# A new order for all 1302 steps of a fused delta-rule attention and bilinear FFN on one core

## The chip, the cores and the metric

One core of a Trainium2 chip runs the whole program. The metric is the device time of one execution in microseconds (us), as the median of several runs. Engines: TensorE (PE; its weight loads are listed as PEld), VectorE (DVE), ScalarE (ACT), GpSimd (POOL) and SyncE (SP), which issues nearly all DMAs.

## The reference: what is computed

Four batches of eight heads, 768 tokens, head size 48, all float32. The first half is a delta rule, token by token; the second half is an FFN whose hidden layer is a product of two projections, without an activation:

```python
for t in range(S):
    kt, vt, bt = (k_n[:, :, t], v[:, :, t], beta[:, :, t, None])
    y[:, :, t] = np.einsum('bhd,bhde->bhe', q[:, :, t], state)
    v_old = np.einsum('bhde,bhd->bhe', state, kt)
    state = state + bt[:, :, :, None] * np.einsum('bhd,bhe->bhde', kt, vt - v_old)
...
a = x @ w1
b = x @ w2
h = a * b @ w3
return (h @ w_out).astype(np.float32)
```

k_n is k divided by its norm. x is y with the heads side by side: 3072 tokens of 384 features; the hidden layer has 1024, and the weights come as 64-bit floats.

## The kernel before, in words

**Tiling.** The tokens of every head are cut into 12 chunks of 64. Within a chunk the recurrence becomes triangular: scores K Kt and K Qt, an inverse of a unit triangular matrix, and products with the state, which is handed from chunk to chunk. Two chunks make a pair j (or group u): their 128 blocks of 32 x 32 are inverted together, and their 512 tokens go through the FFN together. w3 and w_out are multiplied once into one matrix (w34), so the FFN is three products. The second product of the groups and the first two of the last group use a scheme with seven products of half size in place of eight, for which GpSimd forms sums of slabs and of weights.

**Steps.** Each piece of work is a Python generator, and each `yield` ends one step. The text `ORDER` (L39) names generators; a name that stands there for the n-th time runs that generator's n-th step. In this document V0.4 is step 4, counted from 0, of the generator V0. The names:

| name | line | what its steps do |
|---|---|---|
| P0-7, P8-23, P24-35 | L694 | one piece of w_out, of w3, of w1 and w2: .0 a DMA into one of five `raw` buffers (SP), .1 two passes on ACT, .2 two on DVE, .3 one on POOL, by which the 64-bit value becomes float32 |
| t, f | L745, L755 | transposes of w3 (TensorE, then a copy on ACT); products with w_out into w34 |
| k, q, v | L1088 | loads of a chunk; q0 and k0 are issued from ACT's queue, all others from SP's |
| K, Q (chunks 0, 1) | L329 | transposes of k and q on TensorE; copies on ACT and DVE |
| p, d (chunks 2-11) | L222, L318 | loads of k and q in 16 pieces, and their transposes on DVE |
| g, N | L263, L275 | squares of k on POOL and sums on DVE; norms on DVE, with a small product on TensorE |
| s | L356 | scores of a chunk: TensorE, then U and PT on DVE (for chunks 0 and 1 PT goes by ACT and POOL) |
| u | L407 | U to DRAM as blocks, four DMAs |
| V | L419 | a pair's inverse: .0 POOL, .1 load of the blocks (Ub), 31 steps of two DVE instructions each; for pairs 0 and 1 it works in PSUM, with two copies on ACT before (.2, .3; then .4 to .34 on DVE) and after (.35, .36), and .37 stores it |
| e | L475 | the corner blocks of a chunk: .0 loads, .1 DVE, .2 TensorE, .3 ACT, .4 TensorE, .5 ACT |
| n, c | L533, L542 | v times the norm on POOL; the chunk's chain with the state: TensorE and DVE by turns |
| y | L618 | .0 outputs of a chunk on TensorE, .1 copies into xT on ACT, .2 DMAs that fill the last rows of xT |
| b (first half of group 0), a0x to a4x | L771 | FFN, first products: .0 x w1 on TensorE, .1 copy on ACT, .2 x w2 on TensorE, .3 product on DVE |
| S, o, x | L993, L1009, L1059 | sums of slabs (POOL), second product (TensorE), result (ACT, DVE) and its stores (SP) |
| T, W, G5, E5 | L809, L836, L866, L887 | sums of weights (POOL) and of tokens (DVE), and the seven products of the last group |

**What sets the order.** `in_text_order` (L158) ties each engine's instructions to the order in which the list emits them; SP's DMAs too. An engine never overtakes: if the head of its queue waits, all behind it waits. Buffers go round in turn (`in_turn`, L137): five `raw`, four one-bank tiles `ps_f`, two two-bank tiles `ps_w`, three KQ, two xT, and so on; which buffer a step gets, and so whom it waits for, depends on how often the tag was asked for before it. DMAs take eight completion counters in turn, and a DMA waits until the one eight places before it in the list has landed.

Of the kernel before, what the change touches and what calls it, by code (L numbers as in the profile page):

```python
# [48 lines left out]
P30 t12 t14 t15 e0 t15 d3 f7 d3 f6 e0 P30 P21 e0 e0 P24 f7 s2 s2 e1 e0 s2 P24 e0 e1 V1 p4 s2 e1
P26 s2 e1 P25 d3 c0 P21 P30 u2 s3 c0 s3 P26 N1 P31 P24 y0 s3 s3 y0 c0 s3 s3 P25 t13 N1 e1 u3 P31  # L50
c0 P26 P31 P32 c1 V1 c1 e1 P25 V1 P27 c1 V1 c1 V1 V1 t13 V1 V1 V1 V1 V1 V1 y0 V1 P25 f7 f6 f6
P30 P32 P32 v2 V1 P27 s1 P31 V1 V1 y1 b3 b1 V1 b0 P32 P28 y1 b1 V1 b1 b3 P29 P27 b2 b3 y1 V1 P27
b1 b0 P29 P29 c1 a01 b2 a03 P28 V1 a01 a00 b3 P28 P29 a02 a02 a03 P35 P28 V1 a05 b7 a00 V1 V1 V1
V1 a06 P33 V1 b5 a05 b7 b0 V1 P34 V1 b5 V1 a06 V1 V1 V1 P34 k4 V1 P35 V1 g2 a00 V1 k5 a00 b0 V1
V1 g2 a04 P34 n2 p4 n2 a07 c1 a04 b2 b4 P33 b6 b2 P35 V1 g2 g2 P34 g2 e2 a07 g2 P33 e2 P35 c2 c2
e3 d4 a03 d4 a03 a01 P33 g2 b4 d4 g2 e2 b6 e2 a07 e2 b4 d4 T a01 T b4 e2 a07 c2 s4 p5 g2 c2 T g2
N2 V2 b6 p5 b6 s4 b5 s4 c2 a06 c2 a06 a04 v3 y2 d5 b5 d5 k6 s4 e3 d5 s4 y2 a02 a05 d5 s4 b7 a04
n3 S0 a02 a05 S0 s5 S0 u4 e3 s5 n3 s5 e3 b7 T o0 c3 c3 s5 g3 s5 S0 N2 N2 x0 e3 g3 e3 o0 s5 c3 c3
u5 o0 x0 V2 S0 x0 y3 V2 y3 S0 V2 S0 V2 S0 S0 V2 V2 V2 S0 g3 o0 S0 o0 S0 x0 V2 c3 o0 v4 y3 V2 V2
V2 x0 p6 V2 x0 V2 S0 a10 a10 S0 g3 S0 x0 V2 x0 S0 o0 x0 x0 p6 a14 V2 k7 a17 a17 a14 V2 V2 V2 a15  # L60
a16 V2 a16 a15 V2 g3 V2 V2 V2 V2 V2 v5 V2 x0 a13 V2 V2 V2 a17 a12 V2 a13 g3 V2 V2 g3 a17 c3 a14
a13 d6 d6 a11 V2 e4 n4 a12 e4 e4 c4 d6 V3 e4 a14 a10 n4 g3 d6 c4 e5 a11 e4 s6 g3 a13 e4 a12 p7
a10 c4 g3 N3 s6 c4 s6 a11 y4 n5 y4 c4 e5 a12 c4 a11 a15 c5 n5 e5 p7 a16 d7 d7 d7 d7 o1 c5 v6 a16
k8 g4 g4 e5 g4 p8 a15 g4 s7 s7 S1 e5 s7 S1 e5 x1 s7 s7 S1 s7 c5 o1 s6 S1 u7 c5 o1 s6 s6 u6 S1 S1
V3 S1 y5 c5 c5 V3 V3 V3 V3 V3 o1 S1 x1 k9 S1 y5 S1 y5 o1 S1 S1 x1 x1 V3 S1 S1 V3 c6 V3 S1 S1 V3
d8 o1 x1 x1 v7 a20 n6 x1 V3 a20 o1 x1 a23 V3 V3 x1 V3 x1 n7 a27 a24 d8 a26 V3 V3 V3 V3 x1 g4 V3
a23 V3 a25 V3 a27 a27 V3 a24 V3 V3 a26 a20 V3 g4 V3 p8 V3 V3 V3 V3 p9 V3 V3 a25 d8 n6 d8 g4 a20
a22 a22 a24 V3 c6 a27 a25 a24 a21 a21 e6 e6 e6 g4 e7 N3 e6 a25 N3 g4 s8 g4 N4 s8 e6 a22 s8 a26
e6 c6 c6 N4 s8 a26 s8 y6 a22 V4 p9 N4 S2 d9 e7 s8 a21 e7 y6 u8 d9 a21 e7 c6 a23 d9 p10 e7 d9 S2
c6 S2 s9 n7 a23 s9 e7 o2 s9 c7 s9 S2 s9 k10 S2 c7 x2 o2 c7 S2 S2 o2 u9 s9 V4 c7 V4 S2 y7 V4 V4  # L70
x2 V4 g5 g5 V4 p10 d10 y7 S2 x2 S2 o2 y7 V4 o2 x2 c7 V4 V4 S2 S2 V4 o2 a35 x2 x2 k11 x2 S2 V4 x2
S2 a35 v8 V4 S2 V4 V4 S2 V4 x2 n8 o2 a37 x2 V4 v9 V4 V4 V4 x2 a34 n8 V4 V4 a36 a30 V4 V4 V4 V4
V4 a37 V4 a34 a33 V4 g5 a33 a30 a32 a36 V4 V4 V4 V4 a34 a33 V4 V5 a32 e8 n9 c7 e8 a30 c8 a33 e8
e9 e8 g5 a35 a34 c8 a30 e8 g5 d10 a32 e9 g5 a32 g5 a36 e8 e9 S3 c8 a36 a35 a31 d10 d10 e9 a31 n9
c8 g5 c8 c8 g5 g5 e9 a31 s10 N5 e9 p11 s10 s10 a31 c9 a37 a37 p11 c9 y8 N5 v11 d11 S3 d11 d11 o3
v10 d11 s10 y8 s10 S3 u10 S3 s11 N5 s11 o3 s10 c9 s11 c9 s11 S3 x3 S3 s11 o3 S3 S3 y9 o3 s11 x3
S3 o3 u11 V5 S3 S3 V5 y9 V5 x3 n11 S3 x3 V5 V5 V5 S3 y9 S3 S3 V5 c9 V5 o3 x3 V5 x3 x3 V5 V5 x3
S3 a47 o3 x3 V5 V5 a47 x3 V5 V5 a47 n10 V5 a46 a40 a40 V5 a47 V5 a43 V5 a46 x3 a42 a45 V5 a42 V5
a41 a45 a43 V5 V5 V5 V5 V5 V5 a44 V5 a44 V5 a45 a41 V5 V5 V5 V5 c9 W W W W W W W W a42 e10 a40
e10 n11 a42 e10 a44 e10 c10 a45 n10 e11 e10 e11 c10 a43 e10 c10 c10 a40 e11 a41 a46 e11 c10 a44  # L80
S4 a43 e11 a41 S4 c10 o4 e11 a46 c11 x4 S4 S4 y10 o4 c11 c11 S4 y10 S4 S4 S4 S4 S4 c11 o4 y11 o4
x4 S4 S4 S4 o4 y11 x4 x4 o4 S4 x4 x4 S4 y11 S4 x4 G5 x4 E5 x4 o4 x4 E5 x4 E5 E5 S5 E5 E5 S5 E5
E5 S5 o5 S5 S5 S5 o5 S5 S5 S5 x5 S5 S5 S5 o5 o5 x5 S5 S5 S5 o5 S5 o5 x5 x5 o5 x5 x5 x5 x5 x5 x5
x5 x5 x5 x5
"""


# [1117 lines left out]
```

## Time and profile before

| | us |
|---|---|
| median of 3 runs | 587.72 |
| lowest, highest | 586.81, 589.62 |
| the profiled execution's span, first to last instruction | 592.1 |
| TensorE busy in it | 540.8 |
| VectorE, ScalarE, GpSimd busy in it | 378.9, 159.2, 192.8 |

The profiled execution gives no time besides its span, which is 4.4 us above the median of the runs. Its mean granted TensorE clock is 0.971.

When some steps started in it, by matching the trace's instructions with the list:

| step | engine | start, us |
|---|---|---|
| K0.0, first transposes | TensorE | 7.5 (ends 10.9) |
| N0.0, first norms | DVE | 26.3 |
| s1.5, last write of U for pair 0 | DVE | 39.4 |
| V0.4, first step of the first inverse | DVE | 52.2 |
| V0.34, its last; V0.37, its store | DVE; SP | 84.2; 88.4 |
| e0.2, first corner product | TensorE | 97.2 |
| c0.0, first product of the chain | TensorE | 103.8 |
| V1.4, V1.34 | DVE | 125.1, 153.7 |
| e2.2 | TensorE | 165.7 |
| a10.0 | TensorE | 212.4 |
| a23.2 | TensorE | 345.6 |
| W.0, first of the weight sums for the last group | POOL | 476.1 |

How to read a page: busy shares by engine come first, then the span in 40 slices, where a digit is tenths of busy time (PEclk: tenths of the granted clock), then DMA queues, then groups of instructions. A line number is one of the kernel printed above. The waits are given as who waited for whom: total us, how often, and the longest.

### The profile page before, as it was taken

The page shows a single profiled execution, that of the slowest core. Times are in us where ns is not written, and L with a number is a line of the kernel's source. Part 1 is how long each engine was busy: PE and PEld are TensorE (multiplying, and loading weights), DVE is VectorE, ACT ScalarE, POOL GpSimd, SP SyncE. Part 2 cuts the span into 40 slices and gives each one's busy share as a digit, 9 for nine tenths or more (in the row PEclk, how much of TensorE's full clock was granted, in tenths as well). Part 3 has the DMA queues.
Part 4 walks back from the last instruction along what each step waited for, and adds up shares of the span by engine and source line. Part 5 has one row for each costly group of instructions (what it writes and reads, how often), then busy time and mean ns, then how long its engine had stood idle before and what let it go on. Part 6 is the DMA issues. An engine that isn't in the chain of part 4 may idle for free.

```text
span 592.1 us, 19305 instructions
## 1 busy us (share of the span) xinstructions
PE 540.8 (91%) x8268; PEld 393.3 (66%) x8268; DVE 378.9 (64%) x872; ACT 159.2 (27%) x337; POOL 192.8 (33%) x240
## 2 busy tenths in 40 slices
PE   2469889788989999999999989999999999999997
PEld 2456455667878874558854659644688445988897
DVE  3796897678986579674787544874855943325432
ACT  4666354453412202121210222011122112311100
POOL 7563543032453701207121025022051071501441
PEclk9879998779999999999999989999999999999999
DMA  9979997677857445563453344625332040010001
GB/s 245 198 163 268 196 182 140 127 162 154 133 78 101 99 83 107 83 98 56 113 99 75 56 64 86 125 60 78 58 64 79 27 89 4 3 41 27 1 1 53
DMA packets 219508, 57.32 MB, mean 97 GB/s; under 512 B 206656, under 2 KB 212800, under 8 KB 219424
## 3 DMA queue, kind: packets, MB, share of 16 engines
q1 hardware_dynamic: 215232, 55.31, 47.2%
q10 hardware_dynamic: 4192, 0.79, 1.0%
q8 instruction: 65, 1.06, 0.8%
q14 instruction: 19, 0.16, 0.1%
HBM read 43.88 MB, written 11.01 MB: 93 GB/s over the span
## 4 chain that ended last, share of the span: by engine, by line
PE 60%; SPq 15%; DMA 14%; DVE 6%; issue 3%; ACT 1%; POOL 0%; DVEq 0%; ACTq 0%
PE ps_f L778 29%; PE ps_f L1032 14%; SPq L229 6%; PE ps_w L550 4%; DMA raw<-in_moe_w_dram 4%; PE ps_f L897 3%; PE ps_w L651 3%; PE ps_w L897 3%; DMA Ub<-Ud 2%; DMA ktok<-in_k_dram 2%; PE ps_w L497 2%; SPq L201 2%; DMA Ud<-U 2%; DVE tb L439 1%; SPq L683 1%
## 5 line engine op out<-in xcount | busy, mean ns | idle before, releaser
L778 PE MATMUL ps_f<-xT,w2s 128*128 128x512 f32 (+1 forms) x288 | 112.2, 535 | 2.2 <-issue 2.2
L778 PE MATMUL ps_f<-xT,w1s 128*128 128x512 f32 (+1 forms) x288 | 107.0, 524 | 2.8 <-DMA xT<-xT 2.8
L1004 POOL TENSOR_TENSOR ab<-ab 128x256 f32<-128x256 f32 x96 | 67.0, 728 | 90.2 <-DVE ab L794 60.9
L778 PEld LDWEIGHTS ps_f<-xT,w1s 128*128 128x128 f32 x288 | 53.9, 190 | 48.7 <-issue 42.9
L778 PEld LDWEIGHTS ps_f<-xT,w2s 128*128 128x128 f32 x288 | 53.4, 191 | 44.6 <-issue 41.5
L1032 PE MATMUL ps_f<-w,ab 128*128 128x192 f32 x376 | 66.6, 330 | 0.2 <-issue 0.2
L1032 PEld LDWEIGHTS ps_f<-w,ab 128*128 128x128 f32 x376 | 61.1, 190 | 3.8 <-issue 2.9
L790 ACT COPY ab<-ps_f 128x512 f32<-128x512 f32 (+1 forms) x48 | 23.6, 517 | 130.9 <-PE ps_f L778 119.6
L439 DVE TENSOR_TENSOR tb<-Vb,Ub 128x31 f32<-128x31 f32 (+15 forms) x124 | 44.8, 361 | 19.6 <-DMA Ub<-Ud 16.3
L1032 PE MATMUL ps_f<-room,ab 128*128 128x192 f32 x272 | 48.0, 329 | 1.0 <-DVE room L1063 0.8
L444 DVE TENSOR_TENSOR Vb<-Vb,tb 128x31 f32<-128x31 f32 (+15 forms) x124 | 45.0, 363 | 4.3
L758 PE MATMUL ps_f<-w2s,w3T 128*128 128x384 f32 x128 | 45.8, 513 | 0.2 <-ACT w3T L752 0.2
L1032 PEld LDWEIGHTS ps_f<-room,ab 128*128 128x128 f32 x272 | 44.1, 190 | 1.8 <-issue 1.3
L672 ACT COPY xT<-ps_w 48x256 f32<-48x256 f32 x96 | 30.4, 365 | 55.0 <-PE ps_w L651 54.5
L269 POOL TENSOR_TENSOR sq<-ktok 128x384 f32<-128x384 f32 x24 | 20.7, 868 | 68.6 <-DMA ktok<-in_k_dram 62.3
L794 DVE TENSOR_TENSOR ab<-ab,ps_f 128x512 f32<-128x512 f32 (+1 forms) x48 | 27.7, 590 | 16.9 <-PE ps_f L778 16.7
L536 POOL TENSOR_TENSOR vtok<-vtok,n 128x384 f32<-128x384 f32 x24 | 20.3, 855 | 50.1 <-DMA vtok<-in_v_dram 50.1
L758 PEld LDWEIGHTS ps_f<-w2s,w3T 128*128 128x128 f32 x128 | 25.0, 201 | 16.9 <-issue 2.4
L366 PE MATMUL ps_w<-KQ 48*64 48x128 f32 x384 | 30.1, 293 | 1.7 <-DVE PT L396 1.7
L372 PE MATMUL ps_w<-KQ 48*64 48x64 f32 x768 | 30.5, 232 | 0.1
L714 POOL TENSOR_TENSOR w<-w,raw 128x512 uint32<-128x512 uint32 x16 | 20.8, 1305 | 27.7 <-ACT raw L707 9.0
L372 PEld LDWEIGHTS ps_w<-KQ 48*64 48x64 f32 x768 | 27.3, 145 | 0.3 <-ACT KQ L346 0.2
(155 smaller groups left out, 782.2 us busy)
## 6 DMA issues: line engine op xcount, KB each, us to landing
raw<-in_moe_w_dram SPq DMA_DIRECT2D x16, 512.0 KB, 6.5
vtok<-in_v_dram SPq DMA_DIRECT2D x24, 192.0 KB, 4.4
raw<-in_moe_w_dram SPq DMA_DIRECT2D x24, 192.0 KB, 4.6
out_dram<-osb SPq DMA_DIRECT2D x46, 96.0 KB, 2.3
ktok<-in_k_dram SPq DMA_DIRECT2D x44, 96.0 KB, 4.2
raw<-in_moe_w_out_dram SPq DMA_DIRECT2D x8, 384.0 KB, 4.4
Ud<-U SPq DMA_DIRECT2D x48, 64.0 KB, 3.2
Ub<-Ud SPq DMA_DIRECT2D x6, 512.0 KB, 3.9
```

The source lines that it names most:

```text
L229: sync.dma_start(out=dst[quarter(2 * e + j), :, :, tb, 0:nd].rearrange("t b a d -> t (b a) d"), in_=src.rearrange("b (a e) t d -> e (b a) ...
L366: pe.matmul(ps[half(z), 0, n : n + 128], lhsT=x[:, 0, :], rhs=x.rearrange("p j t -> p (j t)"), start=True, stop=True,)
L372: pe.matmul(ps[half(z ^ j), 1, n + C * j : n + C * j + C], lhsT=x[:, 0, :], rhs=x[:, j, :], start=True, stop=True,)
L439: dve.tensor_tensor(out=tv, in0=V[:, 0 : s + 1, s : s + 1].to_broadcast([P, s + 1, n]), in1=U[:, s, s + 1 : BS].unsqueeze(1).to_broadcast( ...
L444: dve.tensor_tensor(out=o, in0=o, in1=tv, op=ALU.subtract)
L672: act.copy(out=xT[f, p:NP:2, b : b + NR, cc, :].rearrange("p a r t -> p r a t"), in_=pyv[f, z, b : b + NR],)
L758: pe.matmul(ps[:, 0:DM], lhsT=w3Ts[jc, kc // 4][:, kc % 4 * P : kc % 4 * P + P], rhs=wo[:, kc], start=(kc == 0), stop=(kc == KF - 1),)
L778: pe.matmul(ps[:].rearrange("p b c t -> p b (c t)"), lhsT=w[:, m, js], rhs=x[:, m, :, c0:c1].rearrange("p b c t -> p b (c t)"), start=(m = ...
L794: dve.tensor_tensor(out=t, in0=t, in1=ps, op=ALU.mult)
L897: pe.matmul(acc[i, w, name], lhsT=w12_sums[w][b][:, P * i : P * i + P], rhs=x_sums[u][x], start=new, stop=True, skip_group_check=not new,)
L1004: pool.tensor_tensor(out=o_, in0=x_, in1=y_, op=op)
L1032: pe.matmul(ps[b][:, b, :], lhsT=abs_[u, HF * f + i][:, t0 : t0 + P], rhs=ws_[w][:, i], start=first and i == 0 and (b == 0 or n == "F"), s ...
```

## The change: the list

`ORDER` is replaced by another order of the same 1302 names, each as often as before. Every generator still runs its own steps in their order, so a step of one name never passes another of the same name; what changes is how the 271 generators are interleaved, and with it each engine's queue, the order on SP's and ACT's DMA queues, and which buffer and which counter a step gets. Nothing else in the file differs, except that the list is one line shorter, so that line numbers behind it fall by one.

The beginnings of the two lists, to the start of the first inverse:

```diff
 ORDER = """
-V0 P0 k0 beta P18 P13 P0 P18 P0 P0 P18 P18 g0 P11 beta P13 K0 K0 P11 P10 q0 P10 P3 k1 P11 P13 K0
-beta P12 g0 P3 K0 g0 K0 g0 P13 K1 g0 P8 P12 g0 K1 K1 P11 P9 Q0 Q0 g0 Q0 P10 P12 g0 Q0 Q0 g0 k2
-K1 s0 g0 P9 P10 P8 N0 K1 q1 P2 s0 N0 P3 Q1 s0 P12 p2 g1 Q1 P2 N0 s0 s0 Q1 P9 Q1 P8 Q1 g1 s0 P3
-s0 t2 t2 t3 s1 P5 P8 P2 g1 s1 P2 P1 s1 s1 t3 P9 P5 s1 P4 s1 P5 u0 P5 s1 d2 P1 P4 t1 u1 t0 P6 t4
-P7 t1 t10 P1 t0 t5 V0 t4 P14 g1 V0 P1 t10 P6 f1 t5 V0 d2 P4 P6 V0 V0 V0 P7 V0 P7 V0 P16 P14 V0
...
+P13 q0 k0 K0 P13 g0 Q0 g0 P11 P11 P12 P10 P11 P11 P13 P13 K0 k1 P3 g0 g0 K0 g0 P10 V0 P10 P0 g0
+P12 K0 K0 Q0 Q0 Q0 P12 K1 K1 P10 Q0 s0 P0 P18 P18 P3 P12 t4 P0 g0 g0 t4 P18 P3 P0 K1 beta q1 beta
+P3 g0 K1 g0 beta N0 s0 K1 Q1 Q1 P8 s0 p2 P18 P4 t5 Q1 Q1 P8 P8 P6 t5 k2 Q1 t2 t10 s0 s0 s0 P6 d2
+d2 s1 s0 s1 s1 s1 P6 s1 s1 P8 P1 P4 P1 u0 t3 P1 P1 P6 t2 P2 t3 P4 P4 t10 P9 P9 P9 u1 P7 P2 P2 P2
+P7 N0 P7 P5 P5 P5 V0 V0 V0 t0 V0 V0 V0 V0 N0 V0 V0 P19 P19 P19 P5 g1 V0 V0 f2 P7 f2 P16 p2 P9 V0
...
```

Other places that the prediction speaks of, each engine's steps alone, old list first:

```
SP, up to e0.0     P21.0 P24.0 p3.0 P26.0 p3.1 V0.37 P30.0 e0.0
                   P20.0 P26.0 P21.0 p3.1 V0.37 P30.0 P24.0 e0.0
TensorE, to c0.0   e0.2 f7.1 e0.4 s2.3 e1.2 c0.0
                   f7.1 e0.2 e0.4 s2.3 t13.0 c0.0
SP, up to V1.37    P33.0 P34.0 k4.0 k5.0 p4.1 V1.37
                   v2.0 k4.0 P34.0 P35.0 p4.1 V1.37 k5.0
SP, before y3.2    V2.1 x0.2 v4.0 y3.2 p6.0
                   V2.1 p6.0 y3.2
TensorE, to s7.3   a16.2 o1.0 s7.0 e5.4 s7.3
                   a15.2 e5.4 s7.0 a11.2 s7.3
TensorE, to a23.2  c6.2 N4.1 s8.3 y6.0 a21.2 e7.2 c6.4 a23.2
                   e7.2 N3.1 c6.2 a24.2 c6.4 y6.0 a23.2
SP, before y7.2    V4.1 p10.1 x2.2 y7.2
                   V4.1 v9.0 x2.2 y7.2
POOL, W            all eight before n11.1, n10.1 and S4.0
                   three behind S4.0, five between S4.14 and S4.15
```

## The prediction

> **What bounds the kernel now.** I read the page's busy shares first, then TensorE's own waits, then busy time in stretches, and last the rows around the longest wait of the second half.
>
> ```profile
> span 592.1 us, 19305 instructions
> PE 540.8 (91%) x8268; PEld 393.3 (66%) x8268; DVE 378.9 (64%) x872; ACT 159.2 (27%) x337; POOL 192.8 (33%) x240
> PEclk9879998779999999999999989999999999999999
> q8 instruction: 65, 1.06, 0.8%
> ```
>
> TensorE is busy for 540.8 of 592.1 us. The last row, of the DMA queues, has packets, MB and share. The list changes no instruction, so all that an order can win or lose is in the other 51.3 us and in the slices with a lower granted clock.
>
> ```profile
> 0.00:20.00 20.00, 6.47 (x138) 5.50 (x140) 8.34 (x14) 9.36 (x15) 13.91 (x28) 1.00 1.03 228
> 20.00:40.00 20.00, 12.77 (x350) 11.34 (x342) 18.91 (x40) 12.39 (x22) 11.04 (x10) 0.74 0.87 187
> 160.00:180.00 20.00, 17.85 (x505) 14.95 (x496) 16.85 (x41) 2.41 (x5) 10.15 (x11) 1.00 0.51 78
> 220.00:240.00 20.00, 20.00 (x48) 8.80 (x47) 17.55 (x40) 3.32 (x6) 4.75 (x7) 1.00 0.50 99
> 340.00:350.00 10.00, 7.75 (x139) 3.50 (x137) 5.37 (x8) 2.89 (x8) 2.20 (x3) 0.83 0.53 77
> ```
>
> Columns after the length: busy PE, PEld, DVE, ACT, POOL, clock, DMA share, GB/s. Adding 20 us less PE over the first ten stretches gives 40.8 us of idle before 200 us; 10.5 us are left after it, 4.0 of them the tail. Later stretches are full (20.00 of 20 at 220 to 240) but for single waits. Early, VectorE is as full as TensorE (18.9 of 20 at 20 to 40; 115.3 against 115.9 of the 140 us from 20 to 160), and what TensorE multiplies there comes from it. So two places are priced: the start, along VectorE's chain, and single waits later.
>
> ```profile
> PE ps_f L336 <- DMA ktok<-in_k_dram: 7.4, 4, 4.9
> PE ps_f L778 <- DMA xT<-xT: 2.8, 3, 1.5
> PE ps_f L778 <- issue: 2.2, 1, 2.2
> 342.80 0.58 PE L550 MATMUL ps_w<-X,ktok 64*48 64x48 f32 x35
> 345.62 0.70 PE L778 MATMUL ps_f<-xT,w2s 128*128 128x512 f32 x1 [2.25 <-issue]
> ```
>
> The first block of names is who TensorE waited for; "issue" means for nothing that the profile shows.
>
> **The start, to e2.2.** I write V0.4 for call 4 (from 0) of the step V0. I add the trace's durations step by step in each list's order and follow the queue that is late. First K0.0, which needs k0's four DMAs. DMAs take eight completion counters in turn, and each waits for the one eight places before: P13's, ninth in the old list, started at 4.93, when k0's first had landed at 4.91. In the new list q0 and P13 are ahead, so k0's third DMA waits for P13 and its fourth for q0's second. q0 has k0's bytes and its old place, and k0's last landed at 8.9; with 0.65 us to issue and 4.1 to 5.9 us to land (k0's first and last) k0 is complete at 13.7 to 15.5. If q0 landed in 4.1 us it would be 10.4. I take 14, since the loads now beside it are as many as then; it was 8.9.
>
> VectorE now has g0.1, which needs k0, at its head (it had 3.0 us of weight pieces ahead of K0.1). From g0.0 on POOL (0.8) it starts at 14.9 with 15.9 us of work before N0.0: 30.8 against 26.3. Behind s0.1 stands P8.2, whose ACT half is queued behind s0.2 and two copies (0.6 each): 2.5 us of idling. But s1.5, the last write of U, ends after 25.7 us of VectorE work and not 28.8: 14.9 + 25.7 + 2.5 = 43.1 (40.1 before). On SP u1 stands behind P9.0, whose buffer is free after P8.3, and POOL does P8.3 after s1.3. From s1.1 (41.5) that is 0.6 of ACT, two times 1.3 of POOL and 0.3 of SP: 45.0. With u1's four issues (2.2 as u0's, 4.0 as its own), 1.7 to land and 5.8 from V0.1 to V0.4, V0.4 starts at 54.7 to 56.5, against 52.2; both rows are as near, so I take the middle, 55.6, +3.4.
>
> From there the new list makes it up, because SP is less in the way:
> - V0.4 to V0.34: 32.2 us of work against 30.8 (N0.2 is in it), and 1.6 of waiting as before: ends 89.4, +4.8.
> - V0.37, the store of the inverse, went out 3.8 us after V0.34 because SP was in p3.1 until 88.4. Now only two ACT copies (0.6 each) lie between: 90.8, +2.4.
> - e0.1 ends 12.1 us of VectorE work behind V0.34 (10.9 before), so e0.2 starts at 101.6, +4.4. From e0.2 to c0.0 took 6.6 with f7.1 (2.78) in the middle; without it two ACT pairs (1.2 each) and 0.7 of TensorE leave 5.0: c0.0 at 106.6, +2.8.
> - c0.0 to the end of s3.3 took 9.5, with 2.0 of "issue" before y0.0; 8.2 by the durations: +1.5. Through u3, P27 and V1.1, V1.4 comes at 125.7, +0.6.
> - V1.4 to V1.34 has 26.0 us of work against 27.0, and 2.0 of waiting as before: 153.7. V1.37 waited 3.9 us behind p4.1 with k5 ahead of it; k5 (2.7) is now behind it. But e2.1 ends 12.2 us of VectorE work behind V1.34 (10.3 before): 165.9, and e2.2 starts at 166.0, against 165.7.
>
> TensorE has 126.7 us of work before e2.2 in both lists. So this term is **+0.3 us**; with k0 at 10.4 every number of the chain is some 3 us earlier (-2.7), and if nothing is made up after V0.4 it is +3.4.
>
> **Instruction fetch.** 16,536 records of TensorE and 65 packets of q8 make 254 to a packet. Packets in dense stretches begin 4.3 to 4.6 us apart (98.4, 103.0, 107.3, 111.7, 116.3), some 58 a us. The old list holds 71 a us over 16.3 us of TensorE work from e6.2 to c6.4; behind it is the 2.25 us wait, and the six passes of a23.2 then took 4.54 us where others take 2.77 (clock 0.83 in 340 to 350). In the new list e6.2 to a23.2 has 60 a us. I take the whole, 2.25 + 1.77: **-4.0 us**. Bounds: -4.8 if e3.4's 0.8 goes too, and +4.0 for one new wait of that kind, since e7.2 to y6.0 is still 88 a us over 7.5 us.
>
> [...]
>
> **Single waits later.** y3.2, which makes the last rows of xT, has p6.0 (4.1 us on SP) ahead of it now, but SP waits for nothing there and is through by 203; what counts is that a10.0 now comes 6.3 us of TensorE work after y3.0, not 9.1. y3.2 started 2.0 after y3.0's end, took 3.7 and lands in 2.0: 7.7, so 1.5 us of waiting. For the third group the distance falls from 10.0 to 9.3: +0.3. Before a35 TensorE waited 0.5, with p10.1 ahead of y7.2 on SP; it is behind it now: -0.5. s7.3 waited 0.92 for VectorE with 0.57 us of TensorE work between; now a11.2 (2.77) covers it: -0.9. Together **+0.4**; bounds -1.4 (no xT wait) and +3. The later inverses have windows of TensorE work of 48.6, 53.5, 48.9 and 48.9 us from scores to corner (49.9, 48.6, 47.6, 47.6 before) and 1 to 3 us more VectorE work in them; spare time was 2 to 5 us, so I cost them at nothing, +2 if that cover is gone. W, moved from 476 to just before E5, puts 10.2 us on POOL where it was idle for 29.0 of the 40 us from 500 to 540: nothing.
>
> **Sum.** 0.3 - 4.0 + 0.4 = -3.3 us on 592.1. Unprofiled runs have a median of 587.7, 4.4 less; the change is carried over unscaled: 584.4.
>
> **Rivals.**
> 1. *The wait stays* (the change doesn't do what it says for fetches): "issue" falls elsewhere, or at y6.0 again. For: 88 a us there, and a stretch of 86 a us (c10.4 to y10.0) that passed without a wait, so density alone doesn't decide. Against: 60 instead of 71 over the longer stretch. 0.3 + 0.4: 588.4.
> 2. *Slower: the late first load is not made up.* VectorE's two inverses pass V0.4's +3.4 on to e2.2, and xT's 1.8 come on top, with no fetch gained: +5.2, 592.9. For: VectorE's 115.3 of 140 us. Against: SP's 3.8 and 3.9 us of delay, which are in the trace. It decides from about 90 on: if V0.34 ends later than that and V0.37 more than 3 us behind it.
> 3. *More*: k0 at 10.4 us: -2.7 instead of 0.3: 581.4.
>
> **How the numbers follow.** The forecast with rival 3: 0.46 (0.34 and 0.12). Rival 1: 0.26. Rival 2: 0.28. About 0.5%, 2.9 us, is what a measurement here can tell from no change. The likeliest is 584.4. The lower end adds up the good bounds (-2.7 - 4.8 - 1.4 = -8.9, 578.8) and some 4 us for the idle of the start that I priced by one chain only: 575. The upper end is rival 2 with one unhidden inverse (+2): 595.
>
> **What would show it.** Right: K0.0 ends at 14 to 16, V0.4 starts at 55 to 57, V0.37 goes out within 2 us of V0.34, e2.2 near 166, no "issue" wait near y6.0 and a23.2 at about 2.8 us, an xT wait of 1 to 2 us before a10.0. Wrong: TensorE's idle before 200 us outside 38 to 43 us, or idle after 200 us above 10.5.

## The result, and the profile after

The new list is slower: a median of 611.99 us (606.68 to 613.16, five runs) against 588.87 (586.81 to 589.62, five runs), a ratio of 1.037, 95% interval 1.033 to 1.042. The forecast was 584.4, and its range ended at 595. The profiled execution spans 605.0 us, and is the fastest of the five; the four others span 609.0 to 611.5. One execution in the experiments below, the profiled one of old_to_e2 (917 us at a clock of 0.57), was disturbed and is left out of every ratio.

The page of the new list, in the lines that answer to those shown of before (busy shares, granted clock in 40 slices, the queue of instruction fetches):

```profile
span 605.0 us, 19284 instructions
PE 545.6 (90%) x8268; PEld 393.8 (65%) x8268; DVE 387.6 (64%) x872; ACT 159.1 (26%) x337; POOL 193.2 (32%) x240
PEclk9766999789899999999999999999999999999999
q8 instruction: 65, 1.06, 0.7%
```

The same 8268 matmul records took 545.6 us instead of 540.8, and VectorE's 872 took 387.6 instead of 378.9. So the 12.9 us between the two profiles are 4.8 us of longer TensorE records and 8.1 us of more idling (49.6 us of idle before 200 us, 40.8 before; 9.7 behind it, 10.5 before). That is an account of TensorE's time and not yet of causes. The longer records go with the granted clock: it is 0.50 for 47.8 us in sum, 34.1 before (not counting the end), and its digits fall to 6 and 7 in the second to fourth slice, where before had 8 and 7 in the second and third. The stretches (columns as in the prediction):

```profile
0.00:20.00 20.00, 4.32 (x128) 3.77 (x128) 3.47 (x5) 3.59 (x5) 8.43 (x21) 1.00 0.79 184
20.00:40.00 20.00, 11.26 (x204) 9.77 (x204) 16.17 (x37) 11.18 (x20) 10.67 (x11) 0.57 0.77 164
140.00:160.00 20.00, 15.97 (x128) 12.68 (x127) 15.27 (x39) 9.20 (x22) 5.31 (x5) 0.91 0.72 133
340.00:350.00 10.00, 10.00 (x322) 6.41 (x322) 4.04 (x9) 4.06 (x7) 0.00 (x0) 1.00 0.30 49
```

In the first 20 us VectorE now works 3.47 us (8.34 before) and TensorE 4.32 (6.47). From 20 to 40 the clock is 0.57. 340 to 350, where before had its long wait, is full. TensorE's own waits:

```profile
PE ps_f L335 <- DMA ktok<-in_k_dram: 14.7, 3, 12.9
PE ps_f L335 <- ACT KQ L345: 8.5, 3, 5.0
PE ps_f L777 <- ACT ab L789: 3.4, 2, 2.8
PE ps_f L748 <- issue: 2.6, 1, 2.6
PE ps_w L549 <- issue: 2.3, 1, 2.3
```

The wait for k grew from 7.4 to 14.7 us; the second and third row had no counterpart; "issue" is there again, at other lines. The one at L748 is t10.0's, and it is no wait for nothing: in the list's order of the `ps_f` banks t10.0 gets one that Q1.0 had, and it starts 0.1 us after ACT's second copy of Q1 has ended (41.39 against 41.29). The wait for xT is gone.

Where the time was lost, by start of a step (us); the last column is a second profile of the same list (608.5 us, the run `new_again` below):

| | before | forecast | after | again |
|---|---|---|---|---|
| K0.0, end | 10.9 | 14 to 16 | 17.4 | 17.4 |
| N0.0 | 26.3 | 30.8 | 35.0 | 35.0 |
| s1.5, end | 40.1 | 43.1 | 48.6 | 48.6 |
| V0.4 | 52.2 | 55.6 | 61.4 | 61.1 |
| V0.34, end | 84.6 | 89.4 | 94.4 | 94.2 |
| V0.37 | 88.4 | 90.8 | 95.5 | 95.9 |
| e0.2 | 97.2 | 101.6 | 109.7 | 109.4 |
| c0.0 | 103.8 | 106.6 | 115.6 | 115.3 |
| V1.4 | 125.1 | 125.7 | 135.6 | 137.4 |
| V1.34, end | 154.1 | 153.7 | 166.6 | 168.5 |
| e2.2 | 165.7 | 166.0 | 178.0 | 180.1 |
| span | 592.1 | 588.8 | 605.0 | 608.5 |

9.2 us are lost at V0.4, 12.3 at e2.2, 12.9 at the end: the loss between these two profiles is the start's, and nothing behind it is won or lost on balance. The two profiles of the new list agree within 0.4 us up to c0.0. The old start has a spread of its own: in old_to_e2_b below, the same first 476 names reach V0.4 at 51.7 and e2.2 at 163.5, so that the loss up to e2.2 is 12 to 17 us by the pair of profiles one takes.

The medians differ by more than the two profiles, by 17 to 23 us. A run's time is 1.7 us above its span, so the old list's profile, 592.1, stands for some 593.8, above the five runs given here, and the new list's is the shortest of its five.

### The profile page after: what moved, and what is told of

It is laid out like the page before. It is cut to its first block, busy times and chain, and to the rows that moved or that the text cites. A ratio compares the mean times of both kernels' runs of the same rounds, so it can differ in the third digit from the quotient of the medians.

```text
span 605.0 us, 19284 instructions
## 1 busy us (share of the span) xinstructions
PE 545.6 (90%) x8268; PEld 393.8 (65%) x8268; DVE 387.6 (64%) x872; ACT 159.1 (26%) x337; POOL 193.2 (32%) x240
## 4 chain that ended last, share of the span: by engine, by line
PE 71%; DVE 9%; DMA 6%; SPq 4%; ACT 3%; issue 3%; POOL 1%; POOLq 0%; ACTq 0%; DVEq 0%
PE ps_f L777 29%; PE ps_f L1031 18%; PE ps_w L549 6%; DMA raw<-in_moe_w_dram 4%; PE ps_w L650 4%; PE ps_f L896 3%; PE ps_w L896 3%; PE ps_w L496 3%; PE ps_w L365 2%; DVE tb L438 2%; PE ps_w L371 2%; DVE Vb L443 2%; DMA qperm<-in_q_dram 1%; SPq L697 1%; SPq L228 1%
## 5 line engine op out<-in xcount | busy, mean ns | idle before, releaser
L777 PE MATMUL ps_f<-xT,w2s 128*128 128x512 f32 (+1 forms) x288 | 113.5, 536 | 2.8 <-ACT ab L789 2.8
L777 PE MATMUL ps_f<-xT,w1s 128*128 128x512 f32 (+1 forms) x288 | 108.9, 526 | 2.3 <-ACT w L764 0.7
L777 PEld LDWEIGHTS ps_f<-xT,w1s 128*128 128x128 f32 x288 | 53.8, 191 | 45.9 <-issue 39.5
L438 DVE TENSOR_TENSOR tb<-Vb,Ub 128x31 f32<-128x31 f32 (+15 forms) x124 | 46.2, 373 | 12.7 <-DMA Ub<-Ud 9.3
L757 PE MATMUL ps_f<-w2s,w3T 128*128 128x384 f32 x128 | 48.1, 528 | 6.2 <-POOL w2s L713 4.5
L443 DVE TENSOR_TENSOR Vb<-Vb,tb 128x31 f32<-128x31 f32 (+15 forms) x124 | 47.2, 381 | 4.3
L377 DVE TENSOR_TENSOR U<-ps_w,wt 128x512 f32<-128x512 f32 x24 | 16.6, 690 | 26.3 <-PE ps_w L371 22.0
```

The costliest lines, as they stand in the source:

```text
L438: dve.tensor_tensor(out=tv, in0=V[:, 0 : s + 1, s : s + 1].to_broadcast([P, s + 1, n]), in1=U[:, s, s + 1 : BS].unsqueeze(1).to_broadcast( ...
L443: dve.tensor_tensor(out=o, in0=o, in1=tv, op=ALU.subtract)
L757: pe.matmul(ps[:, 0:DM], lhsT=w3Ts[jc, kc // 4][:, kc % 4 * P : kc % 4 * P + P], rhs=wo[:, kc], start=(kc == 0), stop=(kc == KF - 1),)
L777: pe.matmul(ps[:].rearrange("p b c t -> p b (c t)"), lhsT=w[:, m, js], rhs=x[:, m, :, c0:c1].rearrange("p b c t -> p b (c t)"), start=(m = ...
```

## The experiments

The results are given as ratios to the kernel before, measured beside each, since its own median moved between 589.9 and 592.5.

| run | what | ratio, 95% interval |
|---|---|---|
| new_again | the new list | 1.031, 1.025 to 1.037 |
| old_first_30 | 30 old names first | 1.021, 1.014 to 1.028 |
| old_head_new_rest | 139 old names first (to V0.4) | 1.012, 1.006 to 1.018 |
| old_to_e2, old_to_e2_b | 476 old names first (to e2.2) | 1.0045, 1.001 to 1.008; 1.003, 1.000 to 1.007 |
| new_head_old_rest | 130 new names first (to V0.4) | 1.030, 1.023 to 1.038 |
| k0_first | k0 P13 q0 | 1.030, 1.023 to 1.036 |
| k0_q0_late | and q0 behind P13.1 | 1.028, 1.023 to 1.034 |
| k0_first_q0_sp | k0 first, q0 from SP | 1.026, 1.019 to 1.033 |
| head_pieces_first | and VectorE's pieces first | 1.025, 1.020 to 1.030 |
| loads_ahead | P29.0, P28.0 ahead of y1.2 | 1.029, 1.024 to 1.033 |
| head_and_loads | the last two in one | 1.015, 1.010 to 1.019 |
| new_w3_no_pool | eight GpSimd passes left out | 1.031, 1.028 to 1.035 |
| before_warm | old list, 86 products in idle time | 1.028, 1.023 to 1.033 |
| before_warm_128 | 128 products | 1.013, 1.005 to 1.020 |
| before_shift_88 | 22 small products | 1.023, 1.018 to 1.028 |
| before_warm_aligned | 86 and 42 small ones | 1.006, 1.003 to 1.008 |
| new_shift_88 | new list, 22 small products | 1.048, 1.042 to 1.054 |

### Which part of the list loses

```diff
-ORDER = the new list
+ORDER = the first n names of the old list, then the names left over, in the new list's order
```

(n = 30, 139, 476; new_head_old_rest is the same the other way round, with 130 new names; new_again has the new list.)

> The new list once more, unchanged, for its spread: its profiled execution took 605.0 us, its other four 609.0 to 611.5. If the start decides (the rounds of q0 and k0 on the DMA queues differ from run to run), a second profile differs from the first before V0.4 and is the same length behind it. If something later does, V0.4 starts at 61.4 within 1 us again and the difference lies behind it. Median 607 to 613.

> The first 139 names of the old list (to the start of the first inverse, V0.4), then the rest in the new list's order. Theory 'the start is carried': the late V0.4 (+9.2 us) goes straight through to the end, and what is left is what the new list lost behind it (+3.6 in the two profiles): V0.4 at 52 to 53, span about 596, median 590 to 595. Rival 'the rest loses': most is lost behind V0.4 whatever the start was: V0.4 at 52 to 53, but e2.2 at 172 or later and a median of 600 or more.

> The first 130 names of the new list (to V0.4), then the rest in the old list's order. Theory 'the start is carried': V0.4 at 60 to 62, span about 601, median 597 to 602. Rival 'the old rest makes it up' (what the prediction had assumed of the new one): e2.2 within 4 us of 165.7, median 588 to 592.

> The first 30 names of the old list (the loads of w_out's and w3's first pieces, k0, beta, q0 and k1, and the passes on P0, P18, P11 and P13 that stand ahead of the squares of k), then the rest in the new list's order. Theory 'who stands at VectorE's head': in the new list VectorE's first instruction needs k0 and stands idle for 16.5 us with weight pieces behind it; with the old first names it does 4 to 5 us of them before k0 is there, so V0.4 comes at 52 to 55, and the median at 596 to 601. Rival 'the rest of the head': the order from N0.0 on (P8.2, P1, P4, P9, P2, P7, P5 ahead of V0.4) is late by itself: V0.4 at 57 or later and a median of 603 or more.

> The first 476 names of the old list (to e2.2), then the rest in the new list's order: what the two later terms of the prediction are worth by themselves. Theory 'they hold': -4.0 for the fetch wait before a23.2 and +0.4 for single waits, so about 588 in the profile and a median 2 to 4 us below the kernel before. Rival 'the fetch wait moves': a new wait for nothing of 2.1 to 2.4 us at c10.4 (where the new list has it in three profiles of three) takes half of it back: median within 2 us of before. Rival 'the middle loses more': E5.0 later than 531 and a median above before.

> The same list as old_to_e2 (first 476 names old, then the new order), for its profile: the median there was 2.9 us above before (ratio 1.0045), where the prediction's two later terms gave -3.6. Theory 'the fetch wait moves': no wait before a23.2, a new one of about 2.3 at c10.4, E5.0 within 2 us of 528.5. Rival 'xT and inverses': a10.0, e4.2, e6.2, e8.2 or e10.2 fall behind old by 2 us or more at one place, by a wait for VectorE or a DMA.

Measured. new_again: the two profiles are the same up to V0.4 (61.1), have the same idle time of TensorE (55.3 and 55.4 us without the tail), and differ by 3.4 us of longer TensorE records: the clock was low for 58 us instead of 48, not counting the end (mean granted clocks of 0.952 and 0.961). So the difference lies behind V0.4, as the second expectation had it; that it goes with the clock, neither had.

With more of the old list in front, the loss shrinks step by step: 3.1 to 3.7% for none of it, 2.1% for 30 names, 1.2% for 139, 0.3 to 0.5% for 476. V0.4 comes at 61.4 in the new list, at 53.6 with 30 old names and at 52.8 with 139. So "who stands at VectorE's head" has V0.4 right, if not quite the median (602.1, expected 596 to 601), and "the start is carried" holds for the most part. Not for all: old_head_new_rest's median, 597.9, lies between the two theories (590 to 595; 600 or more), and with the old start the new order still lost 4.4 us more up to e2.2 (170.7 against 165.7), so the rival has a part in that stretch.

new_head_old_rest isn't clean: V0.4 came at 63.5 (60 to 62 expected), the seam put a wait of 11.3 us for a piece of w3 ahead of t1.0, and V0.34 ended 18.7 us late. But of these 18.7 us the old order gave back 1.2 (span 609.6): nothing catches up here.

The rest behind e2.2 gains nothing. old_to_e2_b is the same list as old_to_e2; its profile has no wait before a23.2, but one of 2.07 at c10.4, and spans 589.2, of which 2.2 of the 2.9 us gained are there at e2.2 already, where the order is still the old one. "The fetch wait moves" has the waits right (E5.0, expected within 2 us of 528.5, came at 525.9), and the median is 1 to 3 us above before.

### What loses up to V0.4

> The new list with its first three names turned round: k0 P13 q0 in place of P13 q0 k0. Theory 'load order': k0 lands at 9 to 10 instead of 15.5, everything to V0.4 comes 5 to 6 us earlier (V0.4 at 55 to 57), and the median falls by about as much, to 605 to 607. Rival 'queues': K0.0 ends 5 us earlier, but VectorE and ACT then wait for what stands behind (weight pieces, q0, k1), so that V0.4 stays within 2 us of 61.4 and the median at 610 or above.

> The new list, beginning k0 P13 K0 P13 q0 g0 Q0 in place of P13 q0 k0 K0 P13 g0 Q0: k0 first, and q0 behind ACT's pass on P13, as the old list had it. Theory 'ACT as the issuer' (with q0 and k0 both first, ACT issued until 12.8 us, and its first pass on a weight came at 14.1): ACT starts before 8 us, VectorE works off weight pieces before k0 lands, and V0.4 comes at 53 to 55 (61.4 in the new list, 57.5 with k0 alone put first). Rival 'the order of VectorE': V0.4 stays at 57 to 58, since what waits are the pieces in VectorE's and GpSimd's queues, not the loads. Both: k0 lands at 9 to 11.

> The new list beginning k0 P13 q0, and q0 issued from SP instead of ACT (one word of the code): ACT is free after k0's issues. Theory 'ACT as the issuer': ACT's first pass (P13.1) comes at 6 to 7 us instead of 11.3, VectorE gets P13.2 and P11.2 done before k0 lands and V0.4 starts at 54 to 56 (57.5 with q0 on ACT). Rival 'VectorE's head': g0.1 still stands ahead of P11.2 and P13.2 on VectorE, so nothing is gained by an earlier ACT: V0.4 at 57 to 59.

> k0_first_q0_sp with its first 18 names in another order: k0 P13 q0 P11 P12 P10 P13 P13 P13 P11 P11 K0 g0 g0 P11 Q0 K0 k1, so that VectorE does its passes on P13 and P11 ahead of the first sums of squares instead of behind them. Theory 'VectorE's head': 2.2 to 3.2 us of VectorE's work move into the time in which it waits for k0, and N0.0 and V0.4 come 2 to 3 us earlier than in k0_first_q0_sp (30.0 and 56.0): V0.4 at 53 to 54, median 601 to 604. Rival 'DMA': the pieces land too late (P11 after 9 us) and hold g0.1 up, so that V0.4 stays at 55.5 or later.

```diff
-P13 q0 k0 K0 P13 g0 Q0 g0 P11 P11 P12 P10 P11 P11 P13 P13 K0 k1 ...   (new list)
+k0 P13 q0 K0 P13 g0 Q0 ...                     k0_first; k0_first_q0_sp with q0 issued from SP
+k0 P13 K0 P13 q0 g0 Q0 ...                     k0_q0_late
+k0 P13 q0 P11 P12 P10 P13 P13 P13 P11 P11 K0 g0 g0 P11 Q0 K0 k1 ...   head_pieces_first, q0 from SP
```

The new list's first 15 us on ACT, issues (ACTq) and work:

```profile
0.81 1.46 ACTq L211 DMA_DIRECT2D X<-in_q_dram  x2
2.29 10.49 ACTq L200 DMA_DIRECT2D ktok<-in_k_dram  x4
12.81 1.28 ACT L705 ACT_TABLE_LOAD   x1 [12.81 <-DMA X<-in_q_dram]
14.11 0.66 ACT L705 ACTIVATE w<-raw 128x512 f32<-128x512 f32 x1
```

k0's four issues take until 12.8 us (3.6 before). The fourth goes out at 12.18, when q0's second DMA has landed at 12.16, beside four weight loads of 512 KB that SP sends off by 3.5. The first and third took 4.5 and 2.9 us themselves (some 0.65 before) without a wait that the profile names; why is open. ACT is the issuer, so its first pass on a weight starts at 14.1, and the pieces that VectorE did in the empty first 15 us of the old list all come later.

With k0 first it lands at 10.5 (15.5 in the new list), and V0.4 comes at 57.5, just past what "load order" expected; the median, 608.1, is past it too. q0 late on ACT didn't help (58.6): k0 landed at 12.7 (9 to 11 expected), and q0's second issue still held ACT until 12.7, so that run didn't do what it was for. q0 from SP did: ACT's first pass starts at 5.1, V0.4 at 56.0, as "ACT as the issuer" had it. With the passes on P13 and P11 ahead of g0.1, V0.4 comes at 54.6; the theory had 53 to 54, the rival 55.5 or later. So the 9.2 us up to V0.4 are 3.9 for k0's place, 1.5 for q0 on ACT, 1.4 for VectorE's head, and 2.4 that these runs leave, each step from a single profile.

But 6.8 us at V0.4 brought only 0.6 to 1.2% at the end, some 4 to 7 us, and 1.2 to 3.4 us at e2.2. Something between them stops the gain.

### What loses between V0.34 and e2.2

> The new list, with GpSimd's pass (.3, which adds the low bits of a weight) left out for the first eight pieces' worth of w3 columns, jc 0 to 3 (P8 to P15); so those weights lack their low bits. P20 to P23, jc 6 and 7, keep it, and so do w_out, w1 and w2. Theory 'GpSimd and VectorE in each other's way': VectorE's passes on P8 to P15 take 1.1 us each (in the new list's profiles P9, P12 and P15 take 1.1, 1.4 and 1.7), while P20.2, P21.2 and P22.2, whose GpSimd passes are kept, still take 1.9 to 2.5 between V0.34 and e0.1, and V0.34 to e0.2 stays at 15.3 us. Rival 'a fixed price': durations are the same with and without GpSimd beside them, 1.1 to 1.7 for P8 to P15 as before. V0.4 comes 1 to 3 us earlier either way.

> The new list with P29.0 and P28.0 put ahead of y1.2 on SP, as in the old list. In the new list y1.2's DMAs wait on SP for ACT until 141.2, the two loads go out at 145.1 and 147.1, ACT waits 5.0 us for the first, and behind ACT wait TensorE (2.85 us before b0.2) and VectorE (2.68 us inside the second inverse). Theory: both waits go, and V1.34 and e2.2 come 2 to 3 us earlier against c0.0 (50.9 and 62.4 us from c0.0 to V1.34 and to e2.2, 50.3 and 61.9 in the old list); the 3.4 us of half clock behind it go too; median 605 to 608. Rival 'raw buffers': the loads wait on SP for a free buffer and hold y1.2 up, so e2.2 stays where it is and b0.0 gets later.

> head_pieces_first (V0.4 at 54.6, 6.8 us earlier than the new list) and loads_ahead (P29.0 and P28.0 ahead of y1.2 on SP) in one. head_pieces_first reached e2.2 only 1.2 to 3.4 us earlier than the new list's two profiles, and its second inverse took 33.4 us from V1.4 to V1.34 instead of 31.0, with VectorE and TensorE (3.7 us before b0.2) waiting for P29. Theory 'the gain is stopped at these loads': without that wait V1.4 to V1.34 takes 28 to 30 us, e2.2 comes at 171 to 174, and the median is 597 to 601. Rival 'given back to the clock or elsewhere': e2.2 at 175 or later and a median of 602 or more.

```diff
-        pool.tensor_tensor(out=du, in0=du, in1=lo, op=ALU.add)
+        if low:          new_w3_no_pool: a piece of w3 has low = jc < 4, all others low = True
+            pool.tensor_tensor(out=du, in0=du, in1=lo, op=ALU.add)
-SP: y0.2 P32.0 y1.2 P29.0 P28.0 P33.0           loads_ahead, head_and_loads
+SP: y0.2 P32.0 P29.0 P28.0 y1.2 P33.0
```

As built, new_w3_no_pool keeps GpSimd's pass for P8 to P15 and leaves it out for P16 to P23: the other half from what its expectation names. So P20 to P22, between V0.34 and e0.1, are the ones without it, and their weights lack the low bits. VectorE behind V0.34 in the new list (two passes of P22.2, two of P21.2), then in new_w3_no_pool:

```profile
94.32 0.42 DVE L708 TENSOR_SCALAR w<-w 128x512 uint32<-128x512 uint32 x1
94.77 1.66 DVE L709 SCALAR_TENSOR_TENSOR w<-raw,w 128x512 uint32<-128x512 uint32 x1
...
96.98 1.27 DVE L708 TENSOR_SCALAR w<-w 128x512 uint32<-128x512 uint32 x1
98.29 1.20 DVE L709 SCALAR_TENSOR_TENSOR w<-raw,w 128x512 uint32<-128x512 uint32 x1
```

```profile
93.64 0.42 DVE L708 TENSOR_SCALAR w<-w 128x512 uint32<-128x512 uint32 x1
94.09 0.69 DVE L709 SCALAR_TENSOR_TENSOR w<-raw,w 128x512 uint32<-128x512 uint32 x1
...
95.81 0.43 DVE L708 TENSOR_SCALAR w<-w 128x512 uint32<-128x512 uint32 x1 [0.41 <-ACT w L705]
96.27 0.69 DVE L709 SCALAR_TENSOR_TENSOR w<-raw,w 128x512 uint32<-128x512 uint32 x1
```

GpSimd's two passes beside the new list's rows:

```profile
94.33 1.55 POOL L713 TENSOR_TENSOR w<-w,raw 128x512 uint32<-128x512 uint32 x1 [9.73 <-DVE tb L438]
96.69 1.28 POOL L713 TENSOR_TENSOR w<-w,raw 128x512 uint32<-128x512 uint32 x1 [0.81 <-ACT w L705]
```

The same instruction takes 0.42 or 1.27, and 0.69 or 1.66. The two long ones, of 1.66 and 1.27, begin while one of GpSimd's passes is under way and end 0.6 and 0.3 us behind its end (95.88 and 97.97). So they may have waited for it rather than run slower; no run separates the two. P22.2, P21.2 and P20.2 took 2.1, 2.5 and 1.9 us in the new list (1.1 each in the old), and 1.1 each without GpSimd; P10.2 and P13.2, whose surroundings were kept, still took 2.2 and 2.1. From the end of V0.34 to e0.1 it is 14.5 us in the new list, 11.1 here, 11.2 in the old. So the longer durations come with GpSimd's passes.

And yet the median stayed at 1.031. e0.2 came 3.9 to 4.1 us earlier than in the new list's two profiles, V1.34 only 0.9 to 2.8, e2.2 0.6 to 2.8. What stops it is seen in the new list's second inverse: SP, ACT and VectorE, one row each and, for ACT, the row ahead of the wait.

```profile
141.19 3.83 SPq L682 DMA_DIRECT2D xT<-xT  x6
145.06 6.77 SPq L697 DMA_DIRECT2D raw<-in_moe_w_dram  x12
```

```profile
145.53 0.92 ACT L789 COPY ab<-ps_f 128x256 f32<-128x256 f32 x3 [1.65 <-PE ps_f L777]
151.46 0.67 ACT L705 ACTIVATE w1s<-raw 128x512 f32<-128x512 f32 x1 [5.01 <-DMA raw<-in_moe_w_dram]
```

```profile
152.16 0.43 DVE L708 TENSOR_SCALAR w1s<-w1s 128x512 uint32<-128x512 uint32 x1 [2.68 <-ACT w1s L705]
```

y1.2 waits on SP until ACT has made xT (141.2), and P29.0 and P28.0, which the old list sent off at 131.9 and 129.7, go out behind it at 145.1. ACT waits 5.0 us for P29, VectorE 2.7 for ACT in the middle of the inverse, and TensorE 2.8 for the copies behind ACT's pass. (In the old list ACT waits 4.8 for P29 as well, but VectorE then only 0.8 and TensorE not at all.) With the two loads ahead of y1.2 these waits of TensorE and VectorE are gone, as is ACT's for P29, and V1.4 to V1.34 takes 29.0 us as in the old list (31.0 and 31.1 in the new one). But V1.4 itself was later, and from c0.0 to e2.2 it took 62.5 us (62.4 and 64.7 in the new list), where 2 to 3 less was expected. By itself that brought some 0.3 to 0.9% (606.7 us, as expected), which is not clear of the noise; the low clock it was to spare went to another place (17 us of it from 111.9 on). With the better head it decided: head_and_loads reaches e2.2 at 171.0, the inverse takes 28.7, and the loss falls from 2.5% to 1.5%. "The gain is stopped at these loads" holds. These edits together take away half of the new list's loss; no version here is faster than the old list.

### Fetches and the clock

> The kernel before, with 86 products of ident with itself put into TensorE's idle time before 43 us (30 ahead of K1.0, 17 in g0, 15 in N0, 24 ahead of t1.0), each into the bank that the step behind it overwrites. Theory 'idle lowers the clock': the stretches of half clock at 25.4 to 35.7 and 42.5 to 45.9 shrink or go, s0.0 takes 1.2 to 1.6 instead of 2.6 and s0.4 1.1 to 1.5 instead of 2.1; V0.4 comes 0 to 1 us earlier, since VectorE sets it, and the median is 0 to 3 us lower. Rival 'the clock goes by time': the same low stretches and durations, and V0.4 0 to 1 us later for the added work.

> before_warm (the old list with 86 extra products in TensorE's idle time, which took V0.4 and e2.2 as early as before but lost 16 us behind it, 14.5 us of it in ten waits for nothing) with 42 more, of 64 x 64, ahead of K0.0: 128 products with 128 weight loads are 256 records, which is what one packet of the instruction queue carries (16,536 records, 65 packets of 16 KB). Theory 'where the blocks fall': the same instructions stand at the ends of blocks as in the kernel before, so the waits for nothing behind 60 us come back to its five places and 5.8 us, and the median is 586 to 592. Rival 'any added work or a faster start makes fetches late': waits for nothing stay at 10 us or more and the median at 600 or above.

> The kernel before with 22 small products (16 x 16) added ahead of the transposes of beta, while TensorE is idle for the loads (0 to 6.1 us): a product leaves two matmul and two weight-load records, so 88 records, a third of a packet of the instruction queue; before_warm had 344 more, which is one packet and 88. Nothing else is changed. Theory 'where the blocks fall': waits for nothing come to about the ten places and 14 us of before_warm, and the median rises by 8 to 15 us. Rival 'the work put into idle time is what made before_warm slow': waits for nothing stay near 5.8 us and the median within 3 us of before.

> before_warm with 42 small products more, ahead of the transposes of beta: 512 extra records, two packets. before_warm_128 had as many, but its 42 stood ahead of K0.0, took 9.1 us and delayed V0.4 by 7.4. Theory 'blocks' and 'idle lowers the clock' together: V0.4 at 51 to 53 as in before_warm, waits for nothing at 4 to 6 us, and a median of 582 to 588, 3 to 8 us below before. Rival 'the gain of before_warm_128 behind V0.4 came from its late start': e2.2 no earlier than 165 and a median of 588 or more.

> The new list with the 22 small products of before_shift_88, here ahead of K0.0, where TensorE is idle until 12.9 us: the blocks of TensorE's instructions are moved by 88 records against the new list as they were against the old one (where it cost 2.3%). Theory 'the old list stood well with its blocks, the new one stands by chance': waits for nothing change places, their sum is between 2 and 10 us and the median is anywhere from 600 to 615, so that the two lists with moved blocks (603.8 for the old one) differ by less than the lists as they are. Rival 'the new list loses the same for other reasons': the median rises by 10 us or more, to 619 or above, as the old list's did.

```diff
+    for _ in range(n): pe.matmul(bank, lhsT=ident, rhs=ident)     ahead of the step that overwrites the bank
     before_warm: K1.0 30, g0 17, N0 15, t1.0 24     before_warm_128: and 42 of 64 x 64 ahead of K0.0
     before_shift_88: 22 of 16 x 16 in beta.1        before_warm_aligned: before_warm and 42 of 16 x 16 in beta.1
     new_shift_88: the new list, 22 of 16 x 16 ahead of K0.0
```

before_warm did in the start what "idle lowers the clock" said: no low clock before 99 us, s0.0 1.25 us instead of 2.61, s0.4 1.20 instead of 2.12, V0.4 at 51.8, e2.2 at 166.1. And then it lost 16 us, with ten waits for nothing that sum to 14.5.

A product in float32 left four records here (two matmuls, two weight loads; the count of records rose by 344 for 86), and I take a packet of q8 to carry 256, an estimate: 65 packets for 16,536 records make 254. By it 344 is one packet and 88 records. So before_shift_88 adds 88 records alone, by 22 small products that run from 1.4 to 2.8 us in an idle TensorE:

```profile
PE ps_w L550 <- issue: 4.2, 4, 1.7
PE ps_w L497 <- issue: 4.1, 3, 1.5
PE ps_w L651 <- issue: 2.8, 3, 1.4
```

Its V0.4 and e2.2 are 2.2 us earlier than before's, its waits for nothing sum to 12 us (5.8 before), and it is 2.3% slower; the profiled execution, 597.8 us, is the fastest of its four, the others took 603.6 to 604.8. With 512 records, two whole packets by that estimate, the longest wait is back at y0.0 (2.1 to 2.2), a23.2's is there again (0.9 to 1.1) beside one at a new place (c1.0 1.4, e11.2 1.3), the sum is 4.8 and 5.6, and the loss 0.6% (before_warm_aligned) and 1.3% (before_warm_128, whose 42 products took 9.1 us and made V0.4 7.4 late). So the theory "where the blocks fall" holds for the waits. Both medians came out above what it gave, 596.4 (586 to 592 expected) and 592.9 (582 to 588).

The places of the waits fit the estimate. Count all 16,702 records of TensorE's queue in the profile of before in order of time, its sequencer's 166 too: the five waits for nothing, of 0.56, 2.00, 0.80, 2.25 and 0.18 us, stand at records 1985, 2241, 5314, 10178 and 12994, each a multiple of 256 behind the first, or one more. In the new list's profile c10.4's, of 2.29 us, stands at 15041, 51 times 256 behind 1985; t10.0's wait for its bank (677) and one of 0.58 us before a22.0 (8835) don't fit. Cut at these places, seven of the old list's 64 stretches of 256 records took under 3.5 us, and five of the seven ended in a wait; of the 57 slower ones none did. In the new list one took under 3.5 us (3.45, no wait). That such a wait is one for fetches is my reading of these places; no row of a trace names it.

The gain that the better clock should have brought (3 to 8 us) didn't come: before_warm_aligned's profile spans 588.5, but its median is 0.6% above before, V0.4 came at 54.2 (51 to 53 expected), and e2.2 at 166.8 is what its rival had. What eats the gain isn't settled.

new_shift_88: the rival holds. Without t10.0's, the waits for nothing rise from 2.9 and 2.4 us to 11.1, and the loss from 3.1 to 3.7% to 4.8%. Unmoved, the new list has fewer of these waits than the old one (5.8), and moving the blocks hurts both, so they aren't what sets the two apart.

## Why the prediction was wrong, step by step

**The failed step is the start: "+0.3 us", bounds -2.7 to +3.4. It was +12.3.** The late first load went through to e2.2 and grew, where the prediction had it made up. The sum was -3.3 us; the profiles differ by +12.9 and the medians by +17 to +23. By its own links:

- k0: taken at 14, bounds 13.7 to 15.5; it landed at 15.5. The wait that counted was read rightly: k0's fourth DMA went out when q0's second had landed (12.18 against 12.16). (The counters go round as SP and ACT issue, not as the names stand in the list: SP's loads behind k0 in the list, issued at 1.24, 1.71 and 2.33, took counters ahead of k0's second DMA, at 6.79.) The mis-sized part was q0, to which I gave the 8.9 us of the old k0: its two DMAs landed at 11.0 and 12.2 beside four weight loads. Rival 3 (k0 at 10.4) was tried by k0_first, 10.5: 3.9 us at V0.4, as priced (3), but under 1% at the end.
- What I didn't price at all: these issues stand on ACT, whose work is queued behind them. k0_first_q0_sp puts 1.5 us on it.
- VectorE to s1.5: its work, 25.7 us, was right to the tenth. Its waits were 6.5 us instead of 2.5: 2.45 for P8.2, as forecast, but also 1.6 for the squares behind P13 on GpSimd, 1.3 for K1 on TensorE, and small ones. Adding up one engine's durations gives the least that its chain can take, and I took it for the time. From u1 to V0.4 it took 11.0, forecast 10.6.
- "From there the new list makes it up, because SP is less in the way": SP did its part. V0.37 went out 1.1 us behind V0.34 (3.8 before, forecast 1.4). But from V0.34's end to e0.1 VectorE took 14.5 us, 11.1 for the same steps without GpSimd's passes (11.2 in the old list): the old list's durations don't hold where GpSimd's passes now stand beside them. And the second inverse took 31.0 from V1.4, forecast 28.0, for the wait behind y1.2. The moves of P28.0 and P29.0 past y1.2 on SP I did not price.
- The clock was in no term of the start, though the profile of before showed 0.74 at 20 to 40. 4.8 us of the 12.9 are longer TensorE records of the same work. Whether they are part of the loss, or fill time in which TensorE would have waited, isn't shown: in before_warm the old start ran without a low clock up to 99 us, and e2.2 came no earlier for it (166.1 against 165.7).

**Fetch, -4.0.** The forecast was right at its place, the term was not: no wait at y6.0, and a23.2 took 2.84 us; from e6.2 to e8.2 the new list needs 75.9 us, the old 78.4. Then 2.3 us were lost at c10.4. Measured over 256 records, from one of the places counted above to the next, the density is another: those up to the old a23.2 took 1.5 us, three such stretches of the new list up to 353.6, ahead of its a23.2, 4.5 to 4.7. Even so it doesn't decide alone: the stretch up to c10.4 took 6.8 us, and with the same names around it, it waits 2.1 to 2.6 us in six profiles and not at all in six others. Rival 1 ("falls elsewhere") has this term.

**Single waits, +0.4.** There was no xT wait before a10.0 (forecast 1.5), no wait at s7.3 (as forecast), and 0.5 in the third group's a32.0 in place of a35. All small. Behind e2.2 the forecast was -3.6 with the fetch term; the new list's two profiles lost 0.6 and 2.0 us there.

**The rivals.** Rival 2 had the sign and the place, and its first test came out (V0.34 at 94.4, later than 90); its second did not (V0.37 1.1 us behind, not 3), and its price, +5.2, was made of the same short chain. The sign set for "wrong" came, too: TensorE's idle before 200 us was 49.6, outside 38 to 43. The range's upper end had no room for a start priced too low at several links at once.

**Left open.** The last 2.4 us up to V0.4; the 0.3 to 0.5% behind e2.2; why c10.4 waits in only half of the profiles; why k0's first and third issue took so long on ACT; and why the medians differ by 4 to 10 us more than the first pair of profiles. The new list's two profiles have the same idle time and differ by 3.4 us of TensorE's records; the old list was profiled a second time only up to e2.2.

## What to carry to other kernels

A list that moves a load or a DMA issue moves all that is queued behind it on the issuing engine (ACT's first pass on a weight at 14.1 us in the new list, at 5.1 in k0_first_q0_sp): walk through each engine's queue, ACT's as well as SP's, before any sum. Durations from one order are no constants in another: with a pass of GpSimd beside it VectorE took 1.27 and 1.66 us for what took 0.42 and 0.69 without, and behind a wait of 2.25 us, at a clock of 0.50 from 346.3 to 349.7, TensorE took 4.54 us for a23.2, 2.84 in the new list. And before two orders with added or removed instructions are compared, count TensorE's records: 88 more, put where TensorE was idle anyway, made a kernel 2.3% slower.

## What the runs showed of the hardware

**Stretches of low clock.** The clock of the two profiles, before and after, is 1.00 or 0.50 throughout. It is 0.50, in us from the span's start and without the end:

| | granted clock 0.50 |
|---|---|
| before | 25.4 to 35.7, 42.5 to 45.9, 90.3 to 93.7, 110.8 to 124.4, 346.3 to 349.7 |
| after | 22.1 to 39.1, 42.5 to 52.8, 56.2 to 63.0, 110.8 to 117.6, 131.3 to 134.7, 155.2 to 158.6 |

Each of the eleven starts in a wait of TensorE's of 1.5 to 5.0 us, or within 1.2 us of its end: 346.3 behind the 2.25 before a23.2, for one, and 131.3 at the end of 2.23 before c1.2. But behind the 2.15 us before e2.2 (165.7) in the old list and the 2.29 before c10.4 (514.7) in the new one the clock stays at 1.00. So such a wait can cost clock or not; a stretch of 3.4 us makes TensorE's work up to 1.7 us longer (an estimate: half of the shortest stretch here). What decides, no run shows, nor why the low clock of new_again, with the same idle time, is 10 us longer in sum. Some records of the first 45 us may be missing: in old_head_new_rest s0.4 takes 2.12 us as in before, with the clock given as 1.00 from 0 to 40.

**Added records.** 88 records moved the two lists' medians by 14 and by 6 to 10 us; 512, with 86 warming products among them, moved the old one's by 3 and 6. In before_shift_88 eleven waits for nothing, of up to 1.7 us each, sum to 12 us; before has five, which sum to 5.8.
